# First part of T as 64x128 matmul pairs, and a new order of the steps, in a two-layer recurrent-memory kernel

## The chip, the cores and the metric

The kernel runs on one core of one Trainium2 chip, in one launch. The metric is the device time of that core in microseconds. A core has five engines that run side by side and meet through semaphores: TensorE (PE; its weight loads are listed apart as PEld), VectorE (DVE), ScalarE (ACT), GpSimd (POOL) and SyncE (SP), which here only issues DMAs.

## The reference

Four blocks in a row over x of shape 1 x 2048 x 448 in bfloat16: attention with a recurrent memory (A), a gated MLP (B), A again, B again, each on the layer norm of x and added to x.

```python
def _A_ref(x, mem0, Wq, Wk, Wv, Wo, seg_len):
    ...
    mem = mem0
    for s in range(n_seg):
        xs = x[:, s * seg_len:(s + 1) * seg_len, :].copy()
        h = jnp.concatenate([mem, xs], axis=1)
        q = jnp.einsum('btd,dhe->bhte', h, Wq)
        k = jnp.einsum('btd,dhe->bhte', h, Wk)
        v = jnp.einsum('btd,dhe->bhte', h, Wv)
        scores = jnp.einsum('bhqe,bhke->bhqk', q, k) * scale
        scores = jnp.where(mask[None, None], scores, -1000000000.0)
        p = _softmax(scores, axis=-1)
        o = jnp.einsum('bhqk,bhke->bhqe', p, v)
        o = jnp.einsum('bhte,hed->btd', o, Wo)
        mem = o[:, :M, :].copy()
        outs.append(o[:, M:, :])

def _B_ref(x, W_gate, W_up, W_down):
    gate = jnp.einsum('bsd,df->bsf', x, W_gate)
    up = jnp.einsum('bsd,df->bsf', x, W_up)
    gate = gate * (lambda x, dt: x.astype(dt))(gate > 0, gate.dtype)
    h = gate * up
    return jnp.einsum('bsf,fd->bsd', h, W_down)

x = x + _A_ref(_layernorm(x, axis=-1), A_mem0, A_Wq, A_Wk, A_Wv, A_Wo, A_seg_len)
x = x + _B_ref(_layernorm(x, axis=-1), B_W_gate, B_W_up, B_W_down)
x = x + _A_ref(_layernorm(x, axis=-1), A_mem0, A_Wq, A_Wk, A_Wv, A_Wo, A_seg_len)
x = x + _B_ref(_layernorm(x, axis=-1), B_W_gate, B_W_up, B_W_down)
```

There are 64 segments of 32 rows, a memory of 8 rows, so 40 keys, and 16 heads. The memory that a segment leaves behind is an input of the next segment: the segments are a chain.

## The kernel before

**Stages.** In a setup (the first 72 us or so) the kernel multiplies each head's Wq with its Wk and its Wv with its Wo. The products M (named Mw; its last 64 rows M3, named M) and N (named Nw) stay in SBUF. After that come 68 steps. Step t works on segment t of the first A and, 4 steps behind (LAG), on segment t-4 of the second A. So 60 steps, 4 to 63, have both layers side by side and move 80 columns (two layers of 40 keys); the four first and the four last have one layer and 40 columns.

**A step.** Its parts, with the names that the order uses:
- `t_block`: T = M times hT, the transposed keys. The 448 rows of the contraction are three tiles of 128 and one of 64. The 64-row tile is the "first" part (t_block0f, t_block1f); the three 128-row tiles are the "rest" (t_block0r.0 to .5, t_block1r.0 to .3). T comes in units of 4 to 6 head slices, each in a PSUM bank of its own. Units go in pairs: block 0 has three pairs of 4, 6 and 5 slices, block 1 two pairs of 5, and block 2 a single unit of 6 without a first part. That is 25 slice pairs in a step. Of a pair, one unit has its 64 rows of M3 in the lower half of the partitions and the other in the upper half (`PLACE`), and hT holds the 64-row tile in both halves. `t_copies` takes each unit out of PSUM, to TTm (memory queries) and TTs (segment queries), on ScalarE or VectorE.
- `s_mem`: scores of the memory queries; a softmax of small operations on VectorE and ScalarE makes Pm. `p_t_mem` transposes it, `u_mem` multiplies with the keys hK to UTm, `un_mem` multiplies with N; ScalarE (sumA) and VectorE (mv, L1176) add the two halves; `m_t` brings the new memory into hT for the next step's `t_block`. This is the chain from step to step.
- `s_seg`: scores of the segment queries and their softmax (L1110 to L1115) to Ps; a DMA transpose makes PTs (L977); `u_seg0` to `u_seg3` multiply with hK and fill U and UTm.
- every second step: `un` multiplies U with N and adds x; the layer norm's result is transposed by DMA to xBT; `b_layer` (gate and up, with its own 64-row first part `b_layerf`) and `b_down` are the MLP.

**Tiling modes.** The matmuls use parts of the array: 128x128 (most), 64x64 (the first part of T in two-layer steps, `b_layerf`, `u_mem`, `u_seg`), 64x128 (the first part of T in one-layer steps), and 128x32 (`un_mem`, `m_t`, some of `un` and `b_down`). The planner counts a change between them as 95 ns.

**The order.** A planner in the program (`_Order`) orders all operations before anything is emitted; each engine then gets its instructions in that order, with semaphore waits where data or banks ask for them. For TensorE, the table `SLOT` gives every operation of a step a due time in ns, in a round of four steps (`PERIOD`, 86000); names end in @0 to @3 for t % 4, and in @a or @z for the first and last four steps. In steps 8 to 63 the slotted operations are chained in exactly the order of their due times. Other engines' operations get their priority from their successors and from `BIAS`. Eight PSUM banks are handed out by the planner, one for each unit or result.

Of the kernel before, what the change touches and what calls it, by code (L numbers as in the profile page):

```python
# [45 lines left out]
class _Sched:  # L46
# [118 lines left out]
    "t_blockm+": 4131, "t_blocks+": 6194, "s_mem+": -350, "p_t_mem+": 7632, "u_mem+": -471, "un_mem+": -457,  # L165
    "un_memh+": -23541, "m_t+": -19808, "m_tk+": -8621, "s_seg+": -19261, "seg_pt+": -2390, "u_seg0+": -23506,
    "u_seg1+": 9252, "u_seg2+": -29593, "u_seg3+": -6650, "m_nat+": 10625, "t_block0f+": 14052, "t_block0r+": -1099,
    "t_block1r+": 22222, "t_block2r+": -17971, "ln_a+": 2217, "ln_ac+": 3345, "un+": -2521, "ln_b+": 1019,
    "b_layer+": -20861, "b_down+": -10132, "m_natx+": 7129, "stay": 2496, "win": 163,
# [5 lines left out]
    "t_block0f.0@a0": 50159, "t_block0r.0@a0": 48445, "t_block0r.1@a0": 66618, "t_block0r.2@a0": 58400,  # L175
    "t_block0r.3@a0": 37177, "t_block0r.4@a0": 67166, "t_block0r.5@a0": 95580, "t_block1f.0@a0": 81552,
    "t_block1r.0@a0": 96466, "t_block1r.1@a0": 76789, "t_block1r.2@a0": 77518, "t_block1r.3@a0": 84652,
    "t_block2r.0@a0": 4656, "s_mem.0@a0": 55973, "fills_mem.0@a0": 52862, "fills_mem.1@a0": 79245,
    "p_t_mem.0@a0": 77938, "u_mem.0@a0": -1119, "fillu_mem.0@a0": 107569, "un_mem.0@a0": 80345, "m_t.0@a0": 42261,
    "s_seg.0@a0": 71567, "u_seg0.0@a0": 100936, "u_seg1.0@a0": 91440, "u_seg2.0@a0": 80408, "u_seg3.0@a0": 56794,  # L180
    "t_block0f.0@a1": 45270, "t_block0r.0@a1": 17400, "t_block0r.1@a1": -7010, "t_block0r.2@a1": 40391,
    "t_block0r.3@a1": 82450, "t_block0r.4@a1": 52995, "t_block0r.5@a1": 62740, "t_block1f.0@a1": 63553,
    "t_block1r.0@a1": 28364, "t_block1r.1@a1": 74689, "t_block1r.2@a1": 76929, "t_block1r.3@a1": 81822,
    "t_block2r.0@a1": 67618, "s_mem.0@a1": 27449, "fills_mem.0@a1": 71144, "fills_mem.1@a1": 63924,
    "p_t_mem.0@a1": 6422, "u_mem.0@a1": 74228, "fillu_mem.0@a1": 51559, "un_mem.0@a1": 53034, "m_t.0@a1": 68700,
    "s_seg.0@a1": 67452, "u_seg0.0@a1": 69786, "u_seg1.0@a1": 83046, "u_seg2.0@a1": 92206, "u_seg3.0@a1": 76576,
    "un0.0@a1": 92765, "un0.1@a1": 79387, "un0.2@a1": 101487, "un0.3@a1": 90435, "un1.0@a1": 63322, "un1.1@a1": 69781,
    "un1.2@a1": 39275, "un1.3@a1": 40361, "un2.0@a1": 106250, "un2.1@a1": 82903, "un2.2@a1": 63137, "un2.3@a1": 42476,
    "un3.0@a1": 64407, "un3.1@a1": 71224, "b_layerf.0@a1": 139224, "b_layer.0@a1": 116387, "b_layer.1@a1": 98718,
    "b_layerf.1@a1": 143708, "b_layer.2@a1": 132409, "b_layer.3@a1": 103128, "b_down.0@a1": 127683,  # L190
    "b_down.1@a1": 126220, "b_down.2@a1": 72769, "b_down.3@a1": 112103, "b_down.4@a1": 96440, "b_down.5@a1": 113434,
    "b_down.6@a1": 125266, "t_block0f.0@a2": 37971, "t_block0r.0@a2": 12506, "t_block0r.1@a2": 60559,
    "t_block0r.2@a2": 46755, "t_block0r.3@a2": 83848, "t_block0r.4@a2": 58924, "t_block0r.5@a2": 46186,
    "t_block1f.0@a2": 28635, "t_block1r.0@a2": 60990, "t_block1r.1@a2": 72547, "t_block1r.2@a2": 53785,
    "t_block1r.3@a2": 60218, "t_block2r.0@a2": 66386, "s_mem.0@a2": 81137, "p_t_mem.0@a2": 78840, "u_mem.0@a2": 59588,
    "un_mem.0@a2": 43030, "m_t.0@a2": 39632, "s_seg.0@a2": 79148, "u_seg0.0@a2": 120824, "u_seg1.0@a2": 115627,
    "u_seg2.0@a2": 122511, "u_seg3.0@a2": 108587, "t_block0f.0@a3": 110070, "t_block0r.0@a3": 140639,
    "t_block0r.1@a3": 112726, "t_block0r.2@a3": 82684, "t_block0r.3@a3": 118188, "t_block0r.4@a3": 132793,
    "t_block0r.5@a3": 95384, "t_block1f.0@a3": 76944, "t_block1r.0@a3": 139308, "t_block1r.1@a3": 124186,
    "t_block1r.2@a3": 80065, "t_block1r.3@a3": 112387, "t_block2r.0@a3": 115734, "s_mem.0@a3": 142810,  # L200
    "p_t_mem.0@a3": 106030, "u_mem.0@a3": 151505, "un_mem.0@a3": 101197, "m_t.0@a3": 76094, "s_seg.0@a3": 97187,
    "u_seg0.0@a3": 127310, "u_seg1.0@a3": 89485, "u_seg2.0@a3": 145237, "u_seg3.0@a3": 114347, "un0.0@a3": 135091,
    "un0.1@a3": 98232, "un0.2@a3": 102557, "un0.3@a3": 118395, "un1.0@a3": 118579, "un1.1@a3": 58610,
    "un1.2@a3": 62740, "un1.3@a3": 81468, "un2.0@a3": 50475, "un2.1@a3": 78517, "un2.2@a3": 78037, "un2.3@a3": 109548,
    "un3.0@a3": 105293, "un3.1@a3": 120353, "b_layerf.0@a3": 53573, "b_layer.0@a3": 80328, "b_layer.1@a3": 92109,
    "b_layerf.1@a3": 63133, "b_layer.2@a3": 92492, "b_layer.3@a3": 34316, "b_down.0@a3": 31797, "b_down.1@a3": 101377,
    "b_down.2@a3": 71871, "b_down.3@a3": 58611, "b_down.4@a3": 86319, "b_down.5@a3": 40731, "b_down.6@a3": 55318,
    "t_block0f.0@0": 33273, "t_block0r.0@0": 36345, "t_block0r.1@0": 33785, "t_block0r.2@0": 35833,
    "t_block0r.3@0": 34297, "t_block0r.4@0": 38392, "t_block0r.5@0": 36857, "t_block1f.0@0": 29690,
    "t_block1r.0@0": 37369, "t_block1r.1@0": 30202, "t_block1r.2@0": 30714, "t_block1r.3@0": 31226,  # L210
    "t_block2r.0@0": 37880, "s_mem.0@0": 39928, "p_t_mem.0@0": 44023, "u_mem.0@0": 45559, "un_mem.0@0": 47607,
    "m_t.0@0": 50678, "s_seg.0@0": 40440, "u_seg0.0@0": 48630, "u_seg1.0@0": 49142, "u_seg2.0@0": 48119,
    "u_seg3.0@0": 51702, "t_block0f.0@1": 55285, "t_block0r.0@1": 57333, "t_block0r.1@1": 56821,
    "t_block0r.2@1": 57845, "t_block0r.3@1": 56309, "t_block0r.4@1": 58357, "t_block0r.5@1": 55797,
    "t_block1f.0@1": 52214, "t_block1r.0@1": 54261, "t_block1r.1@1": 53238, "t_block1r.2@1": 52726,
    "t_block1r.3@1": 54773, "t_block2r.0@1": 53750, "s_mem.0@1": 59380, "p_t_mem.0@1": 61940, "u_mem.0@1": 63476,
    "un_mem.0@1": 70642, "m_t.0@1": 76785, "s_seg.0@1": 59892, "u_seg0.0@1": 69619, "u_seg1.0@1": 70130,
    "u_seg2.0@1": 72178, "u_seg3.0@1": 72690, "un0.0@1": 71154, "un0.1@1": 71666, "un0.2@1": 73202, "un0.3@1": 73714,
    "un1.0@1": 74226, "un1.1@1": 74738, "un1.2@1": 75250, "un1.3@1": 75761, "un2.0@1": 76273, "un2.1@1": 77297,
    "un2.2@1": 77809, "un2.3@1": 78321, "un3.0@1": 78833, "un3.1@1": 79345, "b_layerf.0@1": 86511,  # L220
    "b_layer.0@1": 88047, "b_layer.1@1": 88559, "b_layerf.1@1": 90607, "b_layer.2@1": 87535, "b_layer.3@1": 94190,
    "b_down.0@1": 103404, "b_down.1@1": 103916, "b_down.2@1": 104428, "b_down.3@1": 104940, "b_down.4@1": 105964,
    "b_down.5@1": 108011, "b_down.6@1": 108523, "t_block0f.0@2": 82416, "t_block0r.0@2": 84464,
    "t_block0r.1@2": 82928, "t_block0r.2@2": 83952, "t_block0r.3@2": 86000, "t_block0r.4@2": 83440,
    "t_block0r.5@2": 84976, "t_block1f.0@2": 79857, "t_block1r.0@2": 80880, "t_block1r.1@2": 81904,
    "t_block1r.2@2": 80369, "t_block1r.3@2": 81392, "t_block2r.0@2": 85488, "s_mem.0@2": 87023, "p_t_mem.0@2": 89071,
    "u_mem.0@2": 90095, "un_mem.0@2": 92142, "m_t.0@2": 93678, "s_seg.0@2": 89583, "u_seg0.0@2": 101357,
    "u_seg1.0@2": 106476, "u_seg2.0@2": 101869, "u_seg3.0@2": 107500, "t_block0f.0@3": 97261, "t_block0r.0@3": 98285,
    "t_block0r.1@3": 99309, "t_block0r.2@3": 98797, "t_block0r.3@3": 100333, "t_block0r.4@3": 97773,
    "t_block0r.5@3": 99821, "t_block1f.0@3": 94702, "t_block1r.0@3": 96750, "t_block1r.1@3": 95214,  # L230
    "t_block1r.2@3": 96238, "t_block1r.3@3": 95726, "t_block2r.0@3": 100845, "s_mem.0@3": 102380,
    "p_t_mem.0@3": 105452, "u_mem.0@3": 106988, "un_mem.0@3": 109035, "m_t.0@3": 111595, "s_seg.0@3": 102892,
    "u_seg0.0@3": 109547, "u_seg1.0@3": 110571, "u_seg2.0@3": 110059, "u_seg3.0@3": 111083, "un0.0@3": 112107,
    "un0.1@3": 112619, "un0.2@3": 113130, "un0.3@3": 113642, "un0.4@3": 114154, "un0.5@3": 114666, "un0.6@3": 115178,
# [1210 lines left out]
```

## Time and profile before

| quantity | value |
|---|---|
| time, median of 8 executions | 1537.18 us (1535.04 to 1543.1) |
| the profiled execution's own time | 1537.63 us |
| its span | 1535.8 us |
| instructions | 88464 |
| granted TensorE clock, mean | 0.992 |
| TensorE busy | 1479.8 us, 96% |
| VectorE, ScalarE busy | 803.9, 776.9 us |
| first part of T, 64x64 matmuls | 6000, 77.9 us busy |
| rest of T, 128x128 matmuls of 80 columns | 10080 + 360, 399.8 + 55.2 us busy |

The profile is one execution. Busy time of TensorE is not work at its peak: matmuls are pipelined[...], so the distance from start to start tells what a matmul costs. Almost every TensorE instruction is recorded at one helper line, L139, so groups are told apart by the names of what they write and read (`b` is a PSUM bank) and by shape: 64\*64 is rows by columns of the array, 64x80 the moving operand. "<-issue" after an idle time means that the profile shows no semaphore that ended it.

### The profile page before, as it was taken

The page shows a single profiled execution, that of the slowest core. Times are in us where ns is not written, and L with a number is a line of the kernel's source. Part 1 is how long each engine was busy: PE and PEld are TensorE (multiplying, and loading weights), DVE is VectorE, ACT ScalarE, POOL GpSimd, SP SyncE. Part 2 cuts the span into 40 slices and gives each one's busy share as a digit, 9 for nine tenths or more (in the row PEclk, how much of TensorE's full clock was granted, in tenths as well). Part 3 has the DMA queues.
Part 4 walks back from the last instruction along what each step waited for, and adds up shares of the span by engine and source line. Part 5 has one row for each costly group of instructions (what it writes and reads, how often), then busy time and mean ns, then how long its engine had stood idle before and what let it go on. Part 6 is the DMA issues. An engine that isn't in the chain of part 4 may idle for free.

```text
span 1535.8 us, 88464 instructions
## 1 busy us (share of the span) xinstructions
PE 1479.8 (96%) x41047; PEld 1158.9 (75%) x41051; DVE 803.9 (52%) x2198; ACT 776.9 (51%) x2491; POOL 112.5 (7%) x259
## 2 busy tenths in 40 slices
PE   6999899999999999999999999999999999999998
PEld 2577777778787877878687777878687787878675
DVE  6545545545554555645555555545554554555554
ACT  6634444555545554555545455554555455554433
POOL 4000000000000000000000000000000000000000
PEclk9999999999999999999999999999999999999999
DMA  9740001011110111101110100111010111011010
GB/s 221 183 136 19 17 16 23 21 16 19 22 21 16 24 17 21 23 16 19 21 19 16 27 17 16 22 18 22 16 24 17 22 22 16 18 20 21 20 18 14
DMA packets 137761, 48.24 MB, mean 31 GB/s; under 512 B 125736, under 2 KB 137264, under 8 KB 137392
## 3 DMA queue, kind: packets, MB, share of 16 engines
q1 hardware_dynamic: 137040, 42.33, 14.1%
q8 instruction: 323, 5.29, 1.4%
q14 instruction: 46, 0.38, 0.1%
q10 hardware_dynamic: 352, 0.24, 0.1%
HBM read 10.33 MB, written 1.84 MB: 8 GB/s over the span
## 4 chain that ended last, share of the span: by engine, by line
PE 81%; DMA 6%; DVE 5%; SPq 4%; ACT 3%; issue 1%
PE b L139 81%; SPq L690 3%; DMA PTs<-Ps 2%; DMA xBT<-xn 2%; DVE big L865 2%; ACT UTm L864 1%; ACT Em L1069 1%; DVE UTm L865 1%; DMA xAT<-xn 1%; SPq L1211 1%; DMA ride<-mv 1%; DVE Es L1111 0%; DVE mv L1176 0%; DMA Nw<-in_A_Wo_dram 0%; ACT Es L1112 0%
## 5 line engine op out<-in xcount | busy, mean ns | idle before, releaser
L139 PE MATMUL b<-hT,Mw 128*128 128x80 bf16 (+1 forms) x11424 | 439.2, 200 | 4.5 <-issue 2.9
L139 PEld LDWEIGHTS b<-hT,Mw 128*128 128x128 bf16 x11424 | 418.5, 100 | 18.5 <-issue 6.9
L139 PE MATMUL b<-Nw,big 128*32 128x448 bf16 (+1 forms) x3840 | 294.0, 353 | 2.1 <-DMA Nw<-in_A_Wo_dram 0.9
L864 ACT ACTIVATE TTm<-b 128x80 bf16<-128x80 f32 (+5 forms) x639 | 148.8, 233 | 274.1 <-PE b L139 266.4
L864 ACT ACTIVATE TTs<-b 128x320 bf16<-128x320 f32 (+5 forms) x640 | 269.5, 421 | 5.2 <-PE b L139 4.9
L139 PEld LDWEIGHTS b<-Nw,big 128*32 128x32 bf16 (+1 forms) x3840 | 131.3, 97 | 105.5 <-issue 10.3
L139 PE MATMUL b<-xBT,big 128*128 128x128 bf16 (+3 forms) x4900 | 208.0, 215 | 3.0 <-DMA xBT<-xn 2.6
L139 PE MATMUL b<-Nw,UTm 128*32 128x224 bf16 x7504 | 198.7, 264 | 6.6 <-ACT UTm L864 5.0
L139 PEld LDWEIGHTS b<-Nw,UTm 128*32 128x32 bf16 x7504 | 180.1, 99 | 29.6 <-ACT UTm L864 13.1
L139 PEld LDWEIGHTS b<-xBT,big 128*128 128x128 bf16 (+1 forms) x4900 | 182.7, 101 | 18.0 <-issue 4.1
L865 DVE CAST TTm<-b 64x64 bf16<-64x64 f32 (+4 forms) x245 | 54.5, 223 | 198.5 <-PE b L139 194.3
L139 PE MATMUL b<-hT,M 64*64 64x80 bf16 (+3 forms) x6808 | 146.3, 199 | 2.7 <-issue 1.3
L864 ACT ACTIVATE big<-b 128x512 bf16<-128x512 f32 (+1 forms) x228 | 111.2, 545 | 61.7 <-PE b L139 61.4
L139 PEld LDWEIGHTS b<-hT,M 64*64 64x64 bf16 (+2 forms) x6808 | 110.7, 107 | 27.3 <-issue 18.2
L865 DVE CAST big<-b 128x512 bf16<-128x512 f32 (+1 forms) x160 | 97.4, 624 | 65.0 <-PE b L139 64.4
L864 ACT ACTIVATE UTm<-b 128x512 bf16<-128x512 f32 (+2 forms) x173 | 87.1, 541 | 65.3 <-PE b L139 64.5
L865 POOL COPY hK<-xn 32x448 bf16<-32x448 bf16 x136 | 75.1, 552 | 572.6 <-DVE xn L918 566.3
L865 DVE CAST TTs<-b 64x256 bf16<-64x256 f32 (+5 forms) x244 | 102.5, 420 | 5.3 <-PE b L139 5.3
L1343 DVE TENSOR_TENSOR hB<-gT,b 128x512 bf16<-128x512 bf16 (+2 forms) x128 | 77.9, 619 | 47.9 <-ACT gT L1342 26.6
L139 PE MATMUL b<-big,hB 128*128 128x448 bf16 (+1 forms) x574 | 99.9, 353 | 0.8 <-DVE hB L1343 0.8
L1342 ACT ACTIVATE gT<-b 128x512 bf16<-128x512 f32 (+2 forms) x128 | 66.4, 538 | 64.0 <-DVE hB L1343 34.1
L864 ACT ACTIVATE sumA<-b 64x224 f32<-64x224 f32 x67 | 23.7, 353 | 137.0 <-PE b L139 136.9
(101 smaller groups left out, 1329.2 us busy)
## 6 DMA issues: line engine op xcount, KB each, us to landing
hK<-mv SPq DMA_DIRECT2D x252, 3.5 KB
big<-in_A_Wo_dram SPq DMA_DIRECT2D x3, 896.0 KB, 5.7
ride<-mv SPq DMA_DIRECT2D x124, 7.0 KB, 1.8
out_dram<-ys SPq DMA_DIRECT2D x32, 56.0 KB, 2.0
big<-in_B_W_up_dram SPq DMA_DIRECT2D x7, 224.0 KB, 2.9
big<-in_B_W_gate_dram SPq DMA_DIRECT2D x7, 224.0 KB, 2.7
big<-in_B_W_down_dram SPq DMA_DIRECT2D x7, 224.0 KB, 3.1
XA<-in_A_x_dram SPq DMA_DIRECT2D x28, 56.0 KB, 2.2
```

What stands on the lines that cost most here:

```text
L139: ins = E.matmul(out, lhsT=lhsT, rhs=rhs, **kw)
L690: S.q.add("dma", ("sp",), {"sp": 6200.0 if w == "Wv" and q else 4100.0}, lambda E: E.dma_start_transpose(out=st[w, q], in_=src[w][:, q * 1 ...
L864: return E.activation(out(), src(), ACT.Copy, **({} if scale is None else {"scale": scale}))
L865: return E.tensor_copy(out(), src()) if scale is None else E.tensor_scalar(out(), src(), scale, None, op0=ALU.mult)
L1069: S.act(lambda E, i=i: E.activation(S.Em[:, i, :], src()[:, i, :], ACT.Exp, bias=st[:, 32 + i:33 + i], scale=1.0, accum_out=st[:, 34 + i:3 ...
L1211: S.qdma(f"mk{l}{n}", lambda E, a=a, b=b, n=n: E.dma_start(S.hK[a:a + 8, pp, s, DH * n:DH * n + DH], S.mv[b:b + 8, :]), [("hKm", pp, s, l, ...
L1342: S.act(lambda E, g=g, R=R, n=n: E.activation(S.gT[:, g, 0:n], R[0].b()[:, 0:n], ACT.Relu), n, R[0].res(), [("gT", g)])
L1343: S.dve(lambda E, g=g, R=R, n=n, fcs=fcs: E.tensor_tensor(S.hB[:, fcs[0]:fcs[-1] + 1, 0:w], S.gT[:, g, 0:n].rearrange("p (a b) -> p a b", ...
```

## The change

Two things change.

1. In `t_block`, the first part in two-layer steps used four 64x64 matmuls for a pair of head slices: two column halves for each of the two units. Now it uses two 64x128 matmuls, one for each unit, each with all 128 columns of the stationary tile, as the one-layer steps already did. The products and sums are the same. The mode that the planner is told changes from 3 (64x64) to 1 (64x128).
2. `SLOT` and `BIAS` get new numbers throughout, so the order of TensorE's operations in a round changes in places, as do the priorities on the other engines. `BIAS` loses its entry for u_seg0; "win" and "stay", two weights of the planner's choice, change.

```diff
             for a, b in zip(range(0, len(units), 2), range(1, len(units), 2)):
                 for j in range(units[a][2]):
-                    for o, x in ((0, a), (0, b), (1, a), (1, b)) if l1 - l0 == 2 else ((-1, a), (-1, b)):
+                    for x in (a, b):
                         c, u0, m = units[x]
                         side, slot = S.PLACE[16 * c + u0 + j]
-                        h, g = slice(64 * side, 64 * side + 64), slice(64 * o, 64 * o + 64) if o >= 0 else slice(0, 128)
-                        out.append(MM(R[x].b()[g, j * n:j * n + n], S.M3[h, slot, g], mov(3, h), start=(j == 0), stop=False))
+                        h = slice(64 * side, 64 * side + 64)
+                        out.append(MM(R[x].b()[:, j * n:j * n + n], S.M3[h, slot, :], mov(3, h), start=(j == 0), stop=False))
             return out

         if pair:
-            S.mm(first, sum(u[2] for u in units[::2]) * S.pitch(n) + 25.0, rd, [r for x in R for r in x.res()] + [k for u in units for k in keys(*u)], mode=3 if l1 - l0 == 2 else 1)
+            S.mm(first, sum(u[2] for u in units[::2]) * S.pitch(n) + 25.0, rd, [r for x in R for r in x.res()] + [k for u in units for k in keys(*u)], mode=1)
```

```diff
 BIAS = {
-    "t_blockm+": 4131, "t_blocks+": 6194, "s_mem+": -350, "p_t_mem+": 7632, "u_mem+": -471, "un_mem+": -457,
-    "un_memh+": -23541, "m_t+": -19808, "m_tk+": -8621, "s_seg+": -19261, "seg_pt+": -2390, "u_seg0+": -23506,
...
+    "t_blockm+": -901, "t_blocks+": -588, "s_mem+": -9244, "p_t_mem+": 9533, "u_mem+": -2372, "un_mem+": 5457,
+    "un_memh+": 6866, "m_t+": -46207, "m_tk+": -68429, "s_seg+": -2834, "seg_pt+": -42633, "u_seg1+": 16330,
...
```

Read from `SLOT` by sorting the due times, the order of a round differs in these places (@ is t % 4):

| place | before | after |
|---|---|---|
| step 2, from b_layerf to m_t | b_layerf.0, s_mem@2, b_layer .2 .0 .1, p_t_mem@2, s_seg@2, u_mem@2, b_layerf.1, b_layer .6 .4, un_mem@2, b_layer .5 .7, m_t@2, b_layer.3 | b_layerf.0, s_mem@2, b_layer .2 .0, p_t_mem@2, b_layer.1, u_mem@2, b_layerf.1, b_layer.4, s_seg@2, un_mem@2, b_layer .5 .6, m_t@2, b_layer.3 |
| step 3, from s_mem to p_t_mem | s_mem, s_seg, b_down .0 .1 .2 .3 | s_mem, s_seg, b_down .0 .1, b_layer.7, b_down .2 .3 |
| step 3, between p_t_mem and un_mem | b_down.4, u_seg1@2, u_mem@3, u_seg3@2, b_down .5 .6 | b_down.4, u_seg1@2, u_seg3@2, u_mem@3, b_down .5 .6 |
| step 3, block 2 of T | after block 0 | before block 0 |
| un of step 3, in step 0 | seven of its parts ahead of t_block1f@0 | eight |
| s_mem@1 to p_t_mem@1 | three parts of b_layer between | two |
| rest parts within a block of T | | other permutations |

## The prediction

> **What bounds the kernel now.** I read the page first (busy times, DMA queues), then the groups by shape on TensorE, the waits, the timeline around the longest unexplained pauses, and the instruction counts of single stretches.
>
> ```profile
> PE 1479.8 (96%) x41047; PEld 1158.9 (75%) x41051; DVE 803.9 (52%) x2198; ACT 776.9 (51%) x2491; POOL 112.5 (7%) x259
> ...
> q8 instruction: 323, 5.29, 1.4%
> ...
> PE 81%; DMA 6%; DVE 5%; SPq 4%; ACT 3%; issue 1%
> ```
>
> TensorE is the bound: 96% busy, the other engines near half. The instruction queue moved 323 packets, 5.29 MB, so 16.4 KB each; with 41047 + 41051 TensorE instructions (and some 570 semaphore instructions) that is 256 instructions of 64 bytes per packet.
>
> ```profile
> L139 PE MATMUL b<-hT,Mw 128*128 128x80 bf16 x10080 | 399.8, 202 | 3.3 <-issue 2.9
> L139 PE MATMUL b<-hT,M 64*64 64x80 bf16 x6000 | 77.9, 200 | 1.9 <-issue 1.3 <-DVE hT L865 0.6
> L139 PE MATMUL b<-hT,M 64*128 64x40 bf16 x400 | 7.8, 178 | 0.7 <-DVE hT L865 0.7
> ```
>
> The 6000 matmuls of the second row are what the change halves. The third row is the form they take, so far only in the eight edge steps with 40 columns.
>
> ```profile
> PEld b L139 <- issue: 84.8, 250, 1.0
> PEld b L139 <- DMA PTs<-Ps: 6.6, 9, 1.7
> PEld b L139 <- DMA xBT<-xn: 3.8, 7, 0.9
> ```
>
> Most of the 84.8 us is harmless: weight loads run ahead. The part that stops the matmuls is seen in the timeline of step t%4 = 1:
>
> ```profile
> 676.57 0.67 PE L139 MATMUL b<-hT,Mw 128*128 128x80 bf16 x14
> 677.83 0.73 PE L139 MATMUL b<-hT,Mw 128*128 128x80 bf16 x16 [0.59 <-issue]
> 678.50 0.73 PE L139 MATMUL b<-hT,M 64*64 64x80 bf16 x60
> 679.16 2.04 PE L139 MATMUL b<-hT,Mw 128*128 128x80 bf16 x52
> 681.40 1.29 PE L139 MATMUL b<-hT,Mw 128*128 128x80 bf16 x31 [0.21 <-issue]
> ```
>
> ```profile
> 677.83:681.40 3.57, 3.36 (x128) 3.11 (x128) 0.80 (x3) 2.49 (x10) 0.00 (x0) 1.00 0.49 59
> 765.46:769.19 3.73, 3.36 (x128) 3.11 (x128) 0.43 (x2) 2.30 (x8) 0.00 (x0) 1.00 0.46 57
> ```
>
> Between two such pauses lie 128 matmuls and 128 loads: one packet of instructions. I numbered all TensorE instructions of the trace: over steps 12 to 59 every pause over 60 ns that no semaphore ends sits at the same number modulo 256. They sum to 7.3 us. In the trace a packet's transfer mostly starts within 1.6 us after the packet before it is entered (median 0.64), and no packet ran sooner than 2.2 us after its transfer began. A packet used up in less than some 3.5 us is therefore followed by a pause.
>
> Then the waits that recur in each round of four steps, here in step 3:
>
> ```profile
> 1084.27 2.87 PE L139 MATMUL b<-Nw,UTm 128*32 128x224 bf16 x112 [0.24 <-ACT UTm L864]
> 1087.63 0.95 PE L139 MATMUL b<-PTs,hK 40*64 40x512 bf16 x16 [0.49 <-DMA PTs<-Ps]
> 1088.74 0.27 PE L139 MATMUL b<-selm,mv 128*32 128x16 bf16 x16 [0.16 <-ACT big L864]
> ```
>
> A round takes 87.26 us on average over steps 12 to 59, of which stream and mode drains are some 84.3.
>
> **What the Trainium skill says.** "Runtime: NRT & Kernel Launch", section Instruction fetch mechanics: instructions come in 16 KiB blocks of 256, the next fetched while the current runs. The packets agree; that the fetch is "mostly hidden" does not hold in this kernel's densest stretches. "TensorEngine Tiling (Array Packing)", Key Properties: a change of tiling mode drains TensorE. The trace agrees: from a 128x128 matmul of 80 columns to the first 64x64 one the starts are 132 ns apart instead of 36, so 96 for the drain. The same page, Restrictions: column tiling disables the fast weight load. A 64x64 load takes 108 ns on average, a 64x128 one 93, but loads are ahead of the matmuls, so I price this at nothing.
>
> **The change part by part**, against the profiled execution's own 1537.63 us (span 1535.8, 1.8 around it, 0.45 above the median of 1537.18). A round occurs 15 times in the 60 steps with both layers.
>
> *Array time of the first part of T.* Four 64x64 matmuls of one index start 3, 4, 3 and 26 ns apart: 36 ns. Two 64x128 ones pass the same 80 columns through both row halves; the 128x128 form passes 80 columns in 36 ns, and the edge steps' pairs run at 25.4 ns for 40. I take 36: no gain from half as many matmuls here. Bounds: 33.5 (80 columns at the 0.42 ns by which each further column lengthens the pitch, from 36 ns at 80 to 56.2 at 128 columns of the xBT groups) to 38, so -3.8 to +3 us over 60 x 25 pairs.
>
> *Ends of that part.* A run of 40 64x64 matmuls holds TensorE 485 ns from its first start to the next group's. A 64x128 run of 20 in an edge step holds 350 with 40 columns; nine more pitches of 10.6 and 16.7 more for the last one (40 columns at 0.42) make 462. So -23 ns per run, the same for the run of 60, 120 runs: **-2.7 us** (bounds 0 and -3.6).
>
> *Mode changes.* Sorting the slot tables gives the order of TensorE in a round. Leaving out the transposes of Pm, which show no drain, I count 45 changes before and 46 after: the part used to share the mode of u_seg3 of step 0 and no longer does. 96 ns x 15: **+1.4 us**.
>
> *Instruction supply.* 200 matmuls and 200 loads fewer per round of 4848. Laying the measured durations in both orders, the share of all 256-instruction stretches shorter than 3.5 us falls from 16% to 3%, and the shortfall below 3.5 us from 0.95 to 0.09 us per round. Measured were 7.3 / 12 = 0.61 per round; a tenth stays, so -0.55 x 15: **-8.2 us**. The bounds are 0 and all of it: 7.3 and about 2 at the edges.
>
> *Order.* What I can read from the slots is the TensorE work between producer and consumer. From s_mem to p_t_mem of step 3 it rises from 2.31 to 2.65 us; the Pm chain needs 2.58 there, as its pause of 0.27 each round tells: -0.27. In step 2 the same cover falls from 2.01 to 1.34 (one b_layer part moved behind) and the chain there, which had 0.35 to spare, needs 1.66: +0.32. Together +0.05 x 15: **+0.7 us**. s_seg of step 2 moves about 2.5 us later, just ahead of un_mem: its four VectorE passes of 0.49 us then share the engine with the addition of mv (L1176), behind which m_t and the next step's first part wait, with 0.16 us to spare; a pass caught at the wrong moment costs 0.33. I take 0.05 a round: **+0.7 us** (0 to +5). Its DMA transpose of PTs goes later in SP's queue, ahead of a u_seg that comes some 10 us afterwards: nothing. Its neighbours on that queue (ride and hK, 0.6 us each) keep their order as far as the slots tell. The copies' biases change too; they have no slots, and I take 0 with +-4 us for them and for the edge steps.
>
> *What is late next.* The xBT transpose lands 2.4 us after issue when no instruction packet starts in its way, up to 4.3 when one does; its cover ahead of b_layer's first part is about 3.4. In five of the twelve rounds that cost 0.2 to 0.9 us; in the others the instruction pauses hid it. Taken away, I count 0.24 + 0.12 us per round instead of 0.24, less 0.04 for the longer cover and fewer packets: 0.08 x 15: **+1.2 us**.
>
> Sum: -2.7 + 1.4 - 8.2 + 0.7 + 0.7 + 1.2 = -6.9, so 1530.7 against the own time and 1530.3 against the median: I take 1530.5.
>
> **The rivals.**
>
> *The waits take the pauses' place.* For it: the four rounds from 917 to 1266 us have almost no instruction pauses and still take 87.27 to 87.58 us, with xBT and PTs waits instead; the seven before average 87.28. If all rounds become like those, 87.4: +0.12 for them, -0.18 for the ends, +0.1 for the mode change: +0.04 a round, 1537.8. Against it: in those rounds the packets lay just so that they met the transposes; the round from 480, with neither, took 86.44.
>
> *Slower: Pm of step 2.* The place is p_t_mem of step 2, now with 1.34 us of cover. If its chain, 1.45 us after s_mem's end now, takes the 2.40 that step 3 shows, it costs 0.95 us more, 14.3 us over 15 rounds, and gives 1544.8. It decides from 0.46 us above my 0.32 on. For it: VectorE and ScalarE are half busy, and the slots place b_layer's activations there. Against it: steps 0 and 1 need 1.71.
>
> *More than forecast.* The new order also takes the fixed waits of step 3: 0.31 before un_mem, 0.28 at mv and 0.25 at un: 0.84 x 15 = 12.6, giving 1518. For it: the copies' biases changed most there (m_t, m_tk, seg_pt). Against it: the cover before un_mem and before m_t is the same to 0.1 us.
>
> That the halving does not happen can be left out: the loop says so.
>
> **How the numbers follow.** The forecast has 0.60, more than forecast 0.16, no gain 0.12, slower 0.12. The forecast's own range is 1524 to 1535, from the bounds of the supply, the pairs and the order. To leave out no more than 2 in 10 it reaches to 1518 below and 1538 above. A change of 0.2%, 3 us, is about what a measurement of this kernel can tell from none: faster than 1534 takes the forecast but 0.03 and the third rival, 0.73; within 0.2% the rest of the forecast and most of the first rival, 0.14; slower 0.13.
>
> **What would show it.** In the new profile: 3000 matmuls of 64*128 with 80 columns and none of 64*64 on M; some 299 instruction packets instead of 323 (6000 instructions fewer); pauses marked issue nearly gone from the t_block stretches; 60-matmul runs of 0.66 us start to start become 30-matmul runs of 0.64; a pause of about 0.3 us ahead of the transpose of Pm in step 2 and none in step 3. It is wrong if rounds without instruction pauses take over 87 us, or if pairs take clearly more than 36 ns.

## The result and the profile after

The changed kernel takes **1528.29 us** (median of 12 executions, 1523.09 to 1531.04); the kernel before, run beside it, 1537.63 us (33 executions). The ratio is 0.9934, 95% interval 0.9920 to 0.9948. The forecast was 1530.5. The profiled execution took 1525.29 us, 12.3 less than that of before. Of those, 8.9 lie in the twelve rounds from step 12 to 59 (a round 87.26 -> 86.52 us), 2.7 ahead of them and 0.7 behind.

From the page of the changed kernel: span, busy time by engine, the instruction queue, and the chain that ended last.

```profile
span 1523.5 us, 82670 instructions
...
PE 1473.5 (97%) x38131; PEld 1154.4 (76%) x38135; DVE 793.5 (52%) x2173; ACT 783.1 (51%) x2516; POOL 112.5 (7%) x259
...
q8 instruction: 300, 4.92, 1.3%
...
PE 80%; DVE 8%; DMA 6%; SPq 4%; ACT 2%; issue 1%
```

Nearly 6000 instructions fewer, 300 packets of instructions instead of 323, and TensorE is still the bound. The groups by shape on TensorE:

```profile
L139 PE MATMUL b<-hT,Mw 128*128 128x80 bf16 x10080 | 398.7, 202 | 0.0
...
L139 PE MATMUL b<-hT,M 64*128 64x80 bf16 x3000 | 74.5, 199 | 0.7 <-DVE hT L867 0.6
```

The idle time before the large group was 3.3 us, of which 2.9 ended with "issue". Now it is 0.0. The waits say the same. Here are those of the matmuls themselves in the kernel before (what was waited for; us in total, times, the longest):

```profile
...
PE b L139 <- ACT UTm L864: 5.0, 16, 0.9
PE b L139 <- issue: 4.9, 13, 0.7
...
PE b L139 <- DVE Pm L1073: 3.0, 4, 1.2
...
PE b L139 <- DVE mv L1176: 2.1, 4, 0.9
...
```

and in the changed kernel:

```profile
...
PE b L139 <- DVE mv L1178: 4.5, 15, 0.9
PE b L139 <- DVE Pm L1075: 4.0, 17, 0.7
...
PE b L139 <- ACT UTm L866: 1.6, 2, 0.9
...
```

(The tables of the changed kernel are two lines longer, so L864 and L1176 of before are L866 and L1178 here.) "issue" has gone from 13 waits to a single one of 0.4 us, at 190 us, ahead of the twelve rounds. ScalarE's wait for UTm ahead of un_mem came 16 times and comes twice. In return two waits recur: for Pm (17 times, before 4) and for mv (15 times, before 4). The list counts only the time after a modelled end of the matmul before; the numbers per round below are from start to start, less the usual distance of that place.

The timeline of step t % 4 = 1, the stretch in which the kernel before paused for 0.59 and 0.21 us (start, length, engine, line, operation, how many):

```profile
673.23 1.24 PE L139 MATMUL b<-hT,Mw 128*128 128x80 bf16 x30
674.40 0.71 PE L139 MATMUL b<-hT,M 64*128 64x80 bf16 x30
675.04 3.15 PE L139 MATMUL b<-hT,Mw 128*128 128x80 bf16 x83
```

No bracket with an idle time is left. The run of 30 pairs' matmuls lasts 0.64 us to the next group's start; the run of 60 lasted 0.66.

And the place in step 2 where the order was forecast to cost something, the transposing of Pm:

```profile
707.82 0.28 PE L139 MATMUL b<-xBT,big 128*128 128x128 bf16 x2
708.25 0.23 PE L139 MATMUL b<-ident,Pm 128*128 128x128 bf16 x1 [0.16 <-DVE Pm L1075]
```

The start comes 0.32 us later than after the same work without a wait, in all twelve rounds.

### The profile page after: what moved, and what is told of

Read it like the earlier page. It is cut to its first block, busy times and chain, and to the rows that moved or that the text cites. A ratio compares the mean times of both kernels' runs of the same rounds, so it can differ in the third digit from the quotient of the medians.

```text
span 1523.5 us, 82670 instructions
## 1 busy us (share of the span) xinstructions
PE 1473.5 (97%) x38131; PEld 1154.4 (76%) x38135; DVE 793.5 (52%) x2173; ACT 783.1 (51%) x2516; POOL 112.5 (7%) x259
## 4 chain that ended last, share of the span: by engine, by line
PE 80%; DVE 8%; DMA 6%; SPq 4%; ACT 2%; issue 1%
PE b L139 80%; SPq L692 3%; DMA xBT<-xn 2%; DMA PTs<-Ps 2%; DVE UTm L867 1%; DVE big L867 1%; DMA ride<-mv 1%; SPq L1213 1%; ACT Em L1071 1%; DVE stat L1115 1%; DVE Ps L1117 0%; DVE mv L1178 0%; DVE stat L1112 0%; ACT Es L1114 0%; DVE Es L1113 0%
## 5 line engine op out<-in xcount | busy, mean ns | idle before, releaser
L139 PE MATMUL b<-hT,Mw 128*128 128x80 bf16 (+1 forms) x11424 | 437.7, 200 | 1.2 <-DVE M L867 1.2
L139 PEld LDWEIGHTS b<-hT,Mw 128*128 128x128 bf16 x11424 | 419.6, 100 | 18.0 <-DVE M L867 1.6
L139 PE MATMUL b<-Nw,big 128*32 128x448 bf16 (+1 forms) x3924 | 298.8, 353 | 0.8 <-DMA Nw<-in_A_Wo_dram 0.8
L866 ACT ACTIVATE TTs<-b 128x320 bf16<-128x320 f32 (+5 forms) x666 | 282.1, 424 | 2.6 <-PE b L139 2.5
L866 ACT ACTIVATE TTm<-b 128x80 bf16<-128x80 f32 (+5 forms) x667 | 155.8, 234 | 238.9 <-PE b L139 232.6
L139 PE MATMUL b<-xBT,big 128*128 128x128 bf16 (+3 forms) x4900 | 212.9, 216 | 3.6 <-DMA xBT<-xn 3.2
L139 PEld LDWEIGHTS b<-Nw,big 128*32 128x32 bf16 (+1 forms) x3924 | 129.4, 97 | 99.8 <-issue 10.3
L139 PEld LDWEIGHTS b<-xBT,big 128*128 128x128 bf16 (+1 forms) x4900 | 185.5, 102 | 20.8 <-DMA xBT<-xn 4.6
L139 PE MATMUL b<-Nw,UTm 128*32 128x224 bf16 x7504 | 196.5, 263 | 4.2 <-ACT UTm L866 1.6
L139 PEld LDWEIGHTS b<-Nw,UTm 128*32 128x32 bf16 x7504 | 178.2, 98 | 25.4 <-issue 11.2
L866 ACT ACTIVATE big<-b 128x512 bf16<-128x512 f32 (+1 forms) x214 | 110.1, 566 | 77.6 <-PE b L139 77.1
L867 DVE CAST TTm<-b 64x64 bf16<-64x64 f32 (+5 forms) x217 | 47.4, 219 | 194.7 <-PE b L139 191.8
L139 PE MATMUL b<-hT,M 64*128 64x80 bf16 (+3 forms) x3808 | 141.9, 197 | 1.1 <-DVE hT L867 1.0
L139 PEld LDWEIGHTS b<-hT,M 64*128 64x128 bf16 (+1 forms) x3808 | 105.7, 97 | 27.7 <-issue 10.8
L1344 ACT ACTIVATE gT<-b 128x512 bf16<-128x512 f32 (+1 forms) x128 | 66.8, 543 | 88.0 <-PE b L139 52.0
L866 ACT ACTIVATE UTm<-b 128x512 bf16<-128x512 f32 (+2 forms) x159 | 83.6, 555 | 50.4 <-PE b L139 48.4
L139 PE MATMUL b<-big,hB 128*128 128x448 bf16 (+1 forms) x574 | 100.9, 353 | 0.7 <-DVE hB L1345 0.7
L867 DVE CAST TTs<-b 64x256 bf16<-64x256 f32 (+4 forms) x218 | 88.4, 405 | 2.2 <-PE b L139 2.1
L866 ACT ACTIVATE sumA<-b 64x224 f32<-64x224 f32 x67 | 23.7, 353 | 117.0 <-PE b L139 117.0
```

The lines of the kernel that those rows point to most:

```text
L139: ins = E.matmul(out, lhsT=lhsT, rhs=rhs, **kw)
L866: return E.activation(out(), src(), ACT.Copy, **({} if scale is None else {"scale": scale}))
L867: return E.tensor_copy(out(), src()) if scale is None else E.tensor_scalar(out(), src(), scale, None, op0=ALU.mult)
L1344: S.act(lambda E, g=g, R=R, n=n: E.activation(S.gT[:, g, 0:n], R[0].b()[:, 0:n], ACT.Relu), n, R[0].res(), [("gT", g)])
```

## The experiments

A round of four steps is the measure for most of them: the mean of the twelve rounds from step 12 to 59 in the profiled execution. The medians of executions lie closer together than chance lets them be told apart. One reason is in the profiles: two profiled executions of the same program reached step 12 4 us apart (the changed kernel, 303.4 and 307.3 us) and 7 us apart (the kernel of the third experiment, 312.4 and 305.7), with other waits for transfers in the first 300 us and a granted clock of 0.96 or 0.98 from 72 to 303 us. A round has such a spread too: its two means differ by 0.03 us for the first of these programs and by 0.16 for the second.

The ratios to before are to be read with more care still. The kernel before ran anew beside each group of experiments: its median was 1541.2 us beside experiments 1 to 4 (first runs), 1545.0 beside the repeats of experiment 3 and the first two kernels of experiment 5, and 1536.8 beside its last two. The changed kernel came out at 0.9934 of before in the section above and at 0.9892 in its repeat, with intervals that do not overlap. In that repeat the granted clock of before was 0.992 in the mean of its executions, that of the changed kernel 0.994; this may be part of the difference. So kernels are best compared within a group, and the ratios (which differ from the quotients of the medians by up to 0.2%) not between groups.

**1. The pairs in the order of before.** Is it the form of the matmuls or the order that brings the gain? Only the loop of `t_block` is changed; all engines keep their order.

```diff
-                    for o, x in ((0, a), (0, b), (1, a), (1, b)) if l1 - l0 == 2 else ((-1, a), (-1, b)):
+                    for x in (a, b):
...
-                        h, g = slice(64 * side, 64 * side + 64), slice(64 * o, 64 * o + 64) if o >= 0 else slice(0, 128)
-                        out.append(MM(R[x].b()[g, j * n:j * n + n], S.M3[h, slot, g], mov(3, h), start=(j == 0), stop=False))
+                        h = slice(64 * side, 64 * side + 64)
+                        out.append(MM(R[x].b()[:, j * n:j * n + n], S.M3[h, slot, :], mov(3, h), start=(j == 0), stop=False))
```

> The order of before on every engine, with the first part of T as 64x128 pairs. Instruction supply theory: laying durations in this order, the shortfall of 256-instruction packets below 3.5 us falls from 0.95 to 0.01 us per round, so the 7.3 us of pauses without a semaphore vanish; with ends of runs (-2.7), one drain more per round (+1.4) and xBT waits laid bare (+1.2) it is 8 to 9 us faster than before, about 1529. Rival, the new order made the gain: -2.7 + 1.4, some 1 us faster, about 1536.

Measured: 1528.97 us (6 executions), 0.993 of before (0.9913 to 0.9946), as much as the whole change: the changed kernel with the waits of experiment 4 at its start, which ran in the same group, came to 0.9924. A round takes 86.56 us. The waits of its matmuls:

```profile
PE b L139 <- DMA PTs<-Ps: 5.6, 7, 2.2
...
PE b L139 <- ACT UTm L864: 4.9, 16, 0.9
...
PE b L139 <- DVE Pm L1073: 3.0, 4, 1.2
...
```

The line for "issue" is gone with the form alone, while UTm keeps its 16 waits and Pm its 4: those belong to the order. By instruction number, before had 21 pauses at the packets' boundaries in the twelve rounds, 7.4 us; this kernel has 4, 0.8 us; the changed one 1, 0.1 us.

**2. The order of after with four 64x64 matmuls.** The opposite half: the changed kernel with the loop of before put back (the same lines as above, the other way round).

> The order of the changed kernel on every engine, with the first part of T as four 64x64 matmuls again. Instruction supply theory: the shortfall is 0.91 us per round, the pauses come back at every 256th instruction, 6 to 9 us in all, and with 2.7 for the ends less 1.4 for the shared mode the time is about 1536 to 1538, like before. Rival, the new order made the gain: about 1 us slower than the changed kernel, 1530.

Measured: 1535.85 us (22 executions), 0.9968 of before (0.9955 to 0.9980); a round 87.01 us. In its timeline the pause is back, in the same step:

```profile
502.78 0.73 PE L139 MATMUL b<-hT,M 64*64 64x80 bf16 x60
503.44 1.82 PE L139 MATMUL b<-hT,Mw 128*128 128x80 bf16 x46
505.53 1.16 PE L139 MATMUL b<-hT,Mw 128*128 128x80 bf16 x28 [0.27 <-issue]
```

and in its waits:

```profile
...
PE b L139 <- issue: 4.7, 12, 0.8
PE b L139 <- DVE mv L1178: 4.5, 15, 0.9
PE b L139 <- DVE Pm L1075: 4.3, 18, 0.7
...
PE b L139 <- ACT UTm L866: 1.6, 2, 0.9
...
```

By instruction number there are 23 pauses, 6.5 us, all at the same number modulo 256. So the two parts of the change show apart in the lists: "issue" goes with the form, UTm, Pm and mv with the order. The order alone is worth 0.25 us a round. The two gains don't add up: 0.70 for the form and 0.25 for the order make 0.95, and 0.74 is what both bring. What doesn't add up lies in the waits for the transposes xBT and PTs: 0.50 us a round before, 0.33 with the form alone, 0.29 with the order alone, 0.39 with both. Without them the rounds are 86.76, 86.23, 86.72 and 86.14: 0.53 for the form, 0.05 for the order, 0.63 for both, which agrees to 0.05. These are numbers of one profiled execution each, and a difference of 0.05 is within what a repeat moves. Experiments 4 and 5 ask what moves these waits.

**3. The pause ahead of Pm of step 2.** The new order moved s_seg and b_layer.1 of step 2 out of the stretch between s_mem and p_t_mem. Here both stand in it.

```diff
-    "b_layer.1@1": 88559, "b_layerf.1@1": 89583, "b_layer.2@1": 87023, "b_layer.3@1": 93166, "b_down.0@1": 102380,
+    "b_layer.1@1": 87791, "b_layerf.1@1": 89583, "b_layer.2@1": 87023, "b_layer.3@1": 93166, "b_down.0@1": 102380,
...
-    "un_mem.0@2": 91119, "m_t.0@2": 92654, "s_seg.0@2": 90607, "u_seg0.0@2": 100845, "u_seg1.0@2": 105964,
+    "un_mem.0@2": 91119, "m_t.0@2": 92654, "s_seg.0@2": 88559, "u_seg0.0@2": 100845, "u_seg1.0@2": 105964,
```

> The changed kernel with one move in step 2: b_layer.1 ahead of the transpose of Pm and s_seg right behind it, as before had it. If the 0.32 us pause ahead of that transpose is a lack of cover, it goes in each of some 14 rounds: 4.5 us faster than the changed kernel, about 1524. If something else takes its place (un_mem of step 2 now has 1.29 us of cover against 0.95 needed, or the copies late on their engines), the same as the changed kernel, 1528.

Measured: 1525.67 us (6 executions), 0.9907 of before (0.9884 to 0.9929); a round 86.29 us. The timeline at that place:

```profile
715.83 0.83 PE L139 MATMUL b<-xBT,big 128*128 128x128 bf16 x12
716.50 0.22 PE L139 MATMUL b<-ident,Pm 128*128 128x128 bf16 x1
716.56 0.23 PE L139 MATMUL b<-hT,TTs 128*128 128x40 bf16 x3
```

The transpose follows the xBT matmuls without a wait. To see whether that holds, the same kernel ran a second time beside the changed kernel:

> The changed kernel, unaltered, as the measure for the other three. 1528 us in the median (1525 to 1531), 0.993 of before; a round of four steps 86.5 us; TensorE waits for the DMA transpose xBT or PTs of step 3 in the rounds whose block 1 of T in step 0 stands between about 210 and 60 past a packet's start.

> The changed kernel with s_seg and b_layer.1 of step 2 both ahead of p_t_mem of step 2, a second time beside the changed kernel. If the pause of 0.32 us before p_t_mem of step 2 is worth what it shows: 0.32 x 15 = 4.8 us less than the changed kernel, 1523 to 1525 us. If the gain seen the first time was luck of the packets' places: no more than 1 us less.

Measured: the changed kernel 1526.85 us, 0.9892 of before (0.9868 to 0.9916), a round 86.55; with step 2 reordered 1525.68, 0.9875 (0.9853 to 0.9897), a round 86.45. Both times it is the faster one in the median, but the first time the changed kernel itself ran in another group (the one of experiment 4, in the same group, took 1526.58 us), the second time the intervals overlap, and the gain a round, 0.24 and 0.11 us, is less than the 0.32 that went. The rounds in which no DMA is waited for show where it stands: in the two executions of the changed kernel six of the seven take 86.07 us, and in the two of this one the four take 85.74, 85.74, 85.83 and 86.08 (the last has a pause of 0.32 us at a packet's boundary). The 0.33 is there. What takes part of it back are waits for PTs and xBT: 0.39 and 0.36 us a round in the two executions of the changed kernel, 0.58 and 0.71 in those of this one. So by its rounds without a DMA wait this order is the best of those that ran, with a gain over the changed kernel that its executions don't yet prove.

**4. The packets' places shifted by waits at the start.** Some rounds wait for the DMA transposes xBT and PTs, others don't. In the trace, those that wait have an instruction packet's transfer in the way. If packets cause it, shifting all packet boundaries must move the waits to other rounds. This was tried on the changed kernel with waits on a semaphore that has long been met, ahead of the second group of matmuls:

```diff
-        def run(E):
+        def run(E, pad=ev.n == 2):
             for s, v in waits:
                 E.wait_ge(s, v)
+            for _ in range(PAD if pad else 0):
+                E.wait_ge(*waits[0])
```

> The changed kernel with 128 waits that are already met ahead of the setup's second TensorE group, while the first loads are still under way: half a packet of instructions, nothing else. A round has about 17.5 packets, so packets lie alternately in two places. If waits for xBT in step 1 come from an instruction packet in the transpose's way, they move from every second round to the rounds between, with the same total to 1 us or so. If they come from anything in the order, they stay in the same rounds. Time within 2 us of the changed kernel, plus what the waits cost at the start (0 to 5).

Measured: 1526.58 us (6 executions), 0.9924 of before (0.9905 to 0.9943), a round 86.55. The swap between rounds could not be seen: the 128 waits came out as 64 instructions, two waits in one, so the shift was a quarter of a packet. The xBT of step 3, which step 1 of the next round waits for, was late in rounds 0, 2, 4, 9 and 11, counted from 0; in the changed kernel in 2, 4, 6, 8 and 11. The waits moved, to no list that had been forecast. Inconclusive.

**5. Four places of the packets in one order.** A better base is the kernel of the first experiment. Its round has 4482 TensorE instructions, two rounds 8964, four more than 35 packets, so each place nearly recurs every second round. The same waits at the start, 72 and 200 of them (36 and 100 instructions), shift the places. A place is told as the number of instructions from a packet's start to block 1 of T in step 0.

> The order of before with the pairs, and 36 waiting instructions more on TensorE at its very start, where it waits for the first loads: nothing else is changed, but each later instruction packet begins 36 instructions earlier in the work. A round has 4482 instructions, so two rounds are 4 more than a whole number of packets and the places hold nearly through the run. Theory that packets delay the DMA transposes: with block 1 of T in step 0 now some 198 to 217 and 71 to 92 past a packet's start, hardly a wait for xBT or PTs remains; rounds of 86.2 to 86.3 us instead of 86.56, so some 4 us less than the pairs in the old order had: 1525 us (0.990 of before). Rival, that packets don't matter for the transposes: 1529 us, 0.993.

> As the run before, with 100 waiting instructions instead of 36, so that block 1 of T in step 0 stands some 6 to 25 and 135 to 156 past a packet's start. Theory that packets delay the DMA transposes: waits for xBT or PTs of step 3 in one half of the rounds and for PTs of step 0 or xBT of step 1 in the other, a round of 86.6 to 86.9 us, at least 5 us slower than with 36: 1530 to 1534 us (0.993 to 0.996 of before). Rival: the same as with 36, within 1 us.

Measured: 1530.27 us, 0.9916 (0.9896 to 0.9935), and 1531.74 us, 0.9921 (0.9901 to 0.9941); rounds of 86.70 and 86.75 us. The forecast of 5 us between them fails, and the first has a longer round than the unshifted kernel (86.56) instead of a shorter one. Its rounds say why: at the places 198 and 202 they took 86.23 us, as forecast, but at 206, 210, 214 and 218 they took 87.82, 86.91, 87.47 and 87.57, with waits of up to 1.3 us. The list of good places, taken from other orders, was wrong there. With the places now seen in this order itself, two more shifts were forecast:

> The pairs in the order of before with 16 waiting instructions at the start: block 1 of T in step 0 then stands at 178 to 200 and at 51 to 72 past a packet's start, in turn. Read off the rounds that 0, 36 and 100 such instructions gave at these places: 86.23 us for the first kind, about 86.4 for the second, 86.32 in the mean. Against the pairs with none (86.56) that is 0.24 x 15 = 3.6 us less, and 5.7 us less than with 36 (86.70): 1525 us in the median, at least 5 us under the run beside it. Theory that only chance moves these rounds: the same as the run beside it within 1.5 us.

> The same with 52 waiting instructions: places 214 to 236 and 88 to 108. The earlier rounds at 210 to 218 took 86.9 to 87.6 us, with waits for xBT and PTs of step 3; those at 84 to 92 some 86.3. Mean round about 86.8, the worst of these places: 1532 us, at least 5 us over the run beside it. Theory that only chance moves these rounds: the same within 1.5 us.

Measured in the profiled executions: rounds of **86.33** and **86.71** us (forecast 86.32 and about 86.8), own times 1522.28 and 1528.04 us. The medians are 1526.99 us (0.9932, 0.9911 to 0.9952) and 1526.47 us (0.9933, 0.9917 to 0.9949): no difference at all. The forecast of at least 5 us between the medians fails again. So the places tell which rounds wait in a profiled execution, as forecast to 0.1 us a round (with 52 instructions PTs of step 3 is late in every second round, 0 to 10, by 0.45 to 0.63 us; with 16 in none), and they don't tell the median of executions. Why not stays open; rounds can't be seen in an execution without a profile.

The same transpose, in the fifth of the twelve rounds, in these two kernels. The timeline of the kernel with 16 instructions, of SP and of TensorE (their programs have three lines more, so L139 is L142 and L977 is L980):

```profile
674.04 1.27 SPq L980 DMA_TRANSPOSE xBT<-xn  x1
...
677.16 0.64 PE L142 MATMUL b<-xBT,big 64*64 64x128 bf16 x32
```

and with 52:

```profile
676.50 1.27 SPq L980 DMA_TRANSPOSE xBT<-xn  x1
...
680.59 0.58 PE L142 MATMUL b<-xBT,big 64*64 64x128 bf16 x28 [0.71 <-DMA xBT<-xn]
```

In the trace's list of DMA packets, in the first an instruction packet's transfer starts 2.39 us after the issue and the transpose lands after 2.49; in the second it starts after 1.82 and the transpose lands after 4.04. Nothing else differs between the two programs but the number of waits at the start.

**6. What a round is made of.** The round without a DMA wait, the mean wait for xBT and PTs, and the mean round (us):

| kernel | rounds without | DMA waits | mean round |
|---|---|---|---|
| before | none recurs | 0.50 | 87.26 |
| order of after, 64x64 | none recurs | 0.29 | 87.01 |
| pairs, order of before | 86.24 | 0.33 | 86.56 |
| the same, 36 instructions | 86.23 | 0.55 | 86.70 |
| the same, 100 | 86.24 | 0.63 | 86.75 |
| the same, 16 | 86.24 | 0.06 | 86.33 |
| the same, 52 | 86.23 | 0.60 | 86.71 |
| changed kernel, twice | 86.07 | 0.39, 0.36 | 86.52, 86.55 |
| changed, step 2 reordered, twice | 85.74 | 0.58, 0.71 | 86.29, 86.45 |

The first column is the lowest that comes at least twice in a kernel or its repeat; some rounds without a DMA wait have other delays and lie above it. With 100 instructions it came once (the order is that of the kernels around it). With the pairs, the new order takes 0.17 us off a clean round, and 0.04 and 0.01 of it are left in the two means: the DMA waits are 0.03 to 0.06 longer, other small delays make up the rest. The DMA waits of one and the same order range from 0.06 to 0.63 us with the packets' places, which is more than the new order moves.

## Why the prediction came out

The direction, the mechanism and most terms held; the gain was forecast too small. The forecast sum was -6.9 us; the own times differ by 12.3, the medians by 9.3, and in the repeat by 18 (1545.0 against 1526.9, with the clocks told above). That the first median came so near to 1530.5 is in part luck; the rounds are the better test. By its steps, each in us per round (times 15 for the 60 steps):

- **Instruction supply**: forecast -0.55, measured -0.61 (7.4 to 0.1 us over twelve rounds). Right, and shown from both sides: the pauses go with the pairs alone and come back with the 64x64 form in the new order. The rule behind it, a pause after every packet used up in less than some 3.5 us, was too sharp. In the twelve rounds of before 39 packets were used up in less, and 13 of them were followed by a pause; the other 8 of the 21 pauses followed slower ones. The last section has what the pauses share. The size came out because the forecast scaled the measured 0.61 by the shortfall, and hardly any such packets are left (6 in the changed kernel, none with a pause).
- **Ends of the first part**: a run of 40 became one of 20, 485 to 465 ns (forecast 462); a run of 60 one of 30, 664 to 643. Measured -0.16, forecast -0.18.
- **Array time**: a pair of matmuls starts 3 and 33 ns apart, 36 in sum, as forecast: half as many matmuls, no array time saved.
- **Mode changes**: from u_seg3 of step 0 to the first part of step 1 the distance grew from 123 to 226 ns. Measured +0.10, forecast +0.10.
- **Order, Pm**: the pause of step 3 went from 0.27 to 0, and one of 0.32 came in step 2, both as forecast. The rival that made Pm of step 2 cost 0.95 more falls.
- **Order, the copies**: their biases were taken at 0 with +-4 us. This is the term that was mis-sized. un_mem of step 3 waited 0.31 us for UTm each round and waits 0.13 now, and the rest of step 3 is 0.07 shorter: -0.25 a round, -3.7 us. The timeline of before ahead of un_mem of step 3 (ScalarE and VectorE copy UTm out of PSUM):

```profile
471.34 1.31 ACT L864 ACTIVATE UTm<-b 128x512 bf16<-128x512 f32 x3 [0.46 <-PE b L139]
...
471.83 0.62 DVE L865 CAST UTm<-b 128x448 bf16<-128x448 f32 x1
...
472.70 0.56 PE L139 MATMUL b<-Nw,UTm 128*32 128x224 bf16 x14 [0.24 <-ACT UTm L864]
```

and of after:

```profile
467.41 1.03 ACT L866 ACTIVATE UTm<-b 128x512 bf16<-128x512 f32 x2 [0.46 <-PE b L139]
467.59 0.95 DVE L867 CAST UTm<-b 128x256 bf16<-128x256 f32 x2
...
468.59 0.66 PE L139 MATMUL b<-Nw,UTm 128*32 128x224 bf16 x20
```

  Three copies on ScalarE and one on VectorE became two and two, and the last is done 1.13 us after the first began instead of 1.31: the 0.18 by which the wait shrank. TensorE's slots don't say on which engine a copy runs. What moved this one stays open: the biases and the slots were never changed apart, and the new slots have u_seg3 ahead of u_mem there, so that VectorE's last softmax pass (L1115, in the changed kernel L1117) starts 0.23 to 0.27 us ahead of the first copy instead of 0.09 behind it. The rival "more than forecast" named this wait; a part of it came.
- **s_seg of step 2 and mv**: forecast +0.05. The spare time of m_t of step 2 is 0.22 us before and after: nothing. The wait for mv that the list shows is another one, in step 3 (0.16 to 0.32 a round); it takes the place of a wait for PTs just ahead of it (0.23 to 0.07).
- **xBT laid bare**: forecast +0.08, measured +0.02 (0.245 to 0.264). The mechanism is right, since the clean rounds take 86.07 and the waits make up the rest; its size depends on the packets' places. The rival that waits take the pauses' place completely falls with the two halves: rounds without either take 86.07 to 86.24 us.

The measured terms add up to -0.75 a round, with +0.10 for some small waits for TTm, PTs and hT; the rounds differ by -0.74. Times 15 that is -11.1 us, and the own times' 12.3 holds another 1 or 2 from the edges, where executions of one program differ by more than that.

## What to carry to other kernels

Count instructions as well as array time: where TensorE pauses without a semaphore and the pauses lie a multiple of 256 instructions apart, fewer and larger matmuls pay even when the array passes the same columns in the same time. Test a two-part change in both halves, and set waits that move with something else apart before adding them up: here 0.70 and 0.25 us a round made 0.74. Read the orders of all engines, not of the bound one alone: the largest term missed here came with a copy that changed from ScalarE to VectorE.

## What the runs showed of the hardware

**Instruction packets delay DMA transposes.** Over twelve profiled executions, the PTs transposes in whose way no packet's transfer starts (from 0.6 us before to 2.6 us after the issue) land after 2.42 us, 2.40 to 2.44, 120 of them. Where a packet's transfer starts 0.4 to 0.8 us after the issue, the median landing is 3.3 us; at 0.8 to 1.2 it is 3.5; at 1.2 to 1.6 it is 4.0; at 1.6 to 2.0 it is 4.1 (41 of them, none under 3.9); at 2.0 to 2.4 some take 2.4 and some up to 4.5; from 2.4 to 2.8 it is 2.4 again, with two exceptions. The xBT transposes show the same steps, less sharply (2.42 in the median of 45 with none in the way, the longest 3.15). The shifts of experiment 5, which move nothing but the packets, speak for the packets as the cause. It looks as if the transpose's last part waited behind the packet, which itself mostly takes 0.9 to 1.5 us; that is not shown, and which engine or queue they share was not tried.

**The supply of instructions is not hidden in dense stretches.** The Trainium skill ("Runtime: NRT & Kernel Launch", Instruction fetch mechanics) calls crossing a block of 256 instructions mostly hidden. Here single crossings cost up to 0.80 us in the kernel before, and 0.94 in the second experiment; all of them together 7.4 and 6.5 us in twelve rounds, and 0.1 with some 390 TensorE instructions fewer in a round. What these pauses share is the transfer of the packet that is entered: all 44 ended 1.2 to 1.7 us after it had ended, and no packet of these two kernels was entered sooner than 1.1 us after. In the kernel before, the transfers ahead of the 21 pauses began 0.9 to 2.3 us after the packet before was entered, where the median of all is 0.64: a late transfer counts as well as a dense stretch. Why they begin late was not tried.
